# The head of a delta-rule attention and GELU layer kernel: norms, diagonals, joins, unread products and the order of loads

## The chip, the cores and the metric

The kernel runs on one core of one Trainium2 chip. The metric is device time in microseconds (us), lower is better. An engine is TensorE (PE in the profile; PEld is its weight load), VectorE (DVE), ScalarE (ACT), GpSimd (POOL) or SyncE (SP, here a queue that issues transfers). Each works through its own queue in order; semaphores join them.

## The reference

Two layers follow each other. The first is a delta rule, one state of 48 x 48 for each of 4 batches and 8 heads, over 768 tokens; the second is a dense layer with exact GELU over all 3072 tokens.

```python
k_n = k / (np.linalg.norm(k, axis=-1, keepdims=True) + 1e-06)
for t in range(S):
    kt, vt, bt = (k_n[:, :, t], v[:, :, t], beta[:, :, t, None])
    y[:, :, t] = np.einsum('bhd,bhde->bhe', q[:, :, t], state)
    v_old = np.einsum('bhde,bhd->bhe', state, kt)
    state = state + bt[:, :, :, None] * np.einsum('bhd,bhe->bhde', kt, vt - v_old)
...
x = np.ascontiguousarray(attn_out.transpose(0, 2, 1, 3)).reshape(B * S, H * D)
h = x @ w_in                                      # 3072 x 384 by 384 x 2048
g = 0.5 * h * (1.0 + erf(h / sqrt(2)))
out = g @ w_out                                   # 2048 x 384
```

The weights arrive as 64-bit floats and are rebuilt as 32-bit floats on the chip ("decoding").

## The kernel before

Tokens are taken in 12 chunks of 64. A tile is one chunk of two batches: 128 partitions hold two batches by 64 tokens, and 8 heads lie along the columns. So a chunk c has two tiles (a = 0, 1), and two chunks make a group g with four tiles (numbered t = 0 to 3). Inside a chunk the recurrence is a triangular system. Its matrix is the Gram matrix of the keys, scaled by beta over squared norms. Each 64 x 64 triangle is split into blocks of 32: the two diagonal blocks are inverted by elimination on VectorE, for all heads of a group at once, in thirty row steps (L515 to L530), and the lower left block follows from two small products, the joins (L568).

The head is the code from L201 to L1301. In it, the order of every engine is written out by hand:

- Keys of four tiles are loaded, squared and summed over columns (`squares`, L330), and turned by TensorE (`transposed`, L405), with a copy from PSUM to SBUF on ScalarE (the tile Kt).
- `diagonals` (L476) makes the two 32 x 32 diagonal blocks of each head: 32 products per tile, then one copy to the tile diag.
- `root` (L385) takes a square root on VectorE: a first guess from the bits, then three Newton steps of three operations. `factors` (L322) adds 1e-6, inverts, and makes beta over the squared norm (gm).
- `scales` and `flip` (L495, L506) turn gm and diag so that the row of a block lies along partitions; GpSimd multiplies gm by a triangular mask into the tile XM, and VectorE multiplies the flipped diag by XM (L513).
- While row steps run, TensorE and ScalarE do other preparation: Gram matrices of 16 products per tile (`grams`, L445), turned queries and their products (`queries`, L463), and the same for the third and fourth chunk.
- After the row steps, `back` (L536) turns the result three times: into XM, into the right half of Zf, and into the left half of Zf. `join` (L568) is called for each tile, level 0 (multiplied by gm into XM on VectorE) and level 1 (copied into Zf by ScalarE). `clear` (L552) zeroes the lower left parts of Zf.
- `solve`, `use`, `read`, `turn`, `update` and `next_state` (L779 to L885) compute the first chunk, whose outputs (xT) are what the dense layer multiplies: `fc1` (L909), 16 blocks f of 128 columns of w_in, three products and one GELU each.
- Decoding of one of the 16 weight parts n takes VectorE four or five operations on 768 columns: `begin` (L247: exponent bits), `mantissas` (L269, two operations), `signed` (L276: L281 and L282). Between, ScalarE turns exponent bits into a scale (`exponents`, L258): one Relu, or, where `two_kinks(n)` holds, two Prelus, and then VectorE needs no L281. Parts 0 to 7 are w_in, two blocks f each; parts 8 to 15 are w_out. `fetch` (L223) issues a part's loads; its raw bytes wait in four slots.

From L1316 on, steps get due times by hand (1.05 is 5% into the second unit of the plan) and are emitted in that order; a recording layer keeps VectorE and GpSimd in that order, and `together`, `behind` and `keep` fix parts of TensorE's and ScalarE's. SP issues all loads in the order in which they were written.

Of the kernel before, what the change touches and what calls it, by code (L numbers as in the profile page):

```python
# [19 lines left out]
def kernel(  # L20
# [31 lines left out]
    C = 64  # L52
# [33 lines left out]
    lim = cpool.tile([128, 4], F32)  # L86
    for i, x in enumerate((-896.0 * 2 ** 23, 0.0, -896.0 - 1792.0 / 4095.0, 128.0 * 1792.0 / 4095.0)):
        nc.vector.memset(lim[:, i:i + 1], x)
# [96 lines left out]
    Gp = [cpool.tile([128, NA, NF, 128], F32, name=f"G{i}") for i in range(2)]  # L185
    G = Gp[0]
# [18 lines left out]
    nc.scalar.activation(lim[:, 1:2], lim[:, 0:1], ACT.Gelu)  # L205
# [33 lines left out]
    def two_kinks(n):  # L239

        return 2 < n < n_in or n_in + 3 < n < n_in + 7
# [27 lines left out]
    def mantissas(n):  # L269
        dst, lo, hi, e = halves[n]  # L270
        bits = dst.bitcast(U32)
        nc.vector.tensor_scalar(bits, hi, 0xFFFFF, 0x100000, op0=ALU.bitwise_and,
                                op1=ALU.bitwise_or)
        nc.vector.scalar_tensor_tensor(dst, lo, 2.0 ** -32, bits, ALU.mult, ALU.add)

    def signed(n):  # L276

        dst, lo, hi, e = halves.pop(n)
        scale = high(e, BF16) if two_kinks(n) else e.bitcast(F32)
        if not two_kinks(n):  # L280
            nc.vector.scalar_tensor_tensor(e, hi, 0x80000000, e, ALU.bitwise_and, ALU.bitwise_or)  # L281
        nc.vector.scalar_tensor_tensor(dst, dst, 2.0 ** -20, scale, ALU.mult, ALU.mult)  # L282
        after = n + (NS if n < n_in else len(slots))
        if (after < n_in) == (n < n_in):
            fetch(after)

# [12 lines left out]
    def decode_in():  # L299

        marks = {3: (None, 1.05, 0.99, 1.06), 4: (1.0, 1.09, 1.1, 1.13),
                 5: (1.12, 1.18, 1.14, 1.2), 6: (1.19, 1.24, 1.21, 1.25),
                 7: (1.245, 1.3, 1.29, 1.36)}
        steps = []
        for n, (a, b, c, d) in marks.items():
            if a is not None:
                steps += [(a, (begin, n))]
            steps += [(b, (exponents, n, keep)), (c, (mantissas, n)), (d, (signed, n))]
        return steps
# [75 lines left out]
    def root(x):  # L385

        shape = list(x.shape)
        s = wk.tile(shape, F32, tag="root", name="root", bufs=1)
        r = wk.tile(shape, F32, tag="root_r", name="root_r", bufs=1)
        nc.vector.tensor_scalar(s.bitcast(U32), x.bitcast(U32), 0.5, 532487669.0,  # L390
                                op0=ALU.mult, op1=ALU.add)
        nc.vector.tensor_scalar_mul(x, x, 0.5)
        for i in range(3):
            nc.vector.reciprocal(r, s)
            nc.vector.tensor_tensor(r, r, x, op=ALU.mult)
            nc.vector.scalar_tensor_tensor(x if i == 2 else s, s, 0.5, r, ALU.mult, ALU.add)
# [8 lines left out]
    def transposed(u, part=(0, 1)):  # L405
        for x in part:
            if x == 0:
                dst = u.Kt = wk.tile([128, 2, NP, C], F32, tag="Kt", name="Kt", bufs=6)
            elif u.c == 1:
                dst = u.Qt = su.tile([128, 2, NP, C], F32, tag="Qt1", name="Qt1")  # L410
            else:
                dst = u.Qt = SQ[:, u.a, :, :, D:]
            if x and u.c == 3:
                psT = dn("psT")[:, 0].rearrange("q (j n) -> q j n", n=128)
            else:
                psT = sq("psT", NP, 128)
            flat = (Qp[2 + u.a] if u.c == 3 and x == 0 else (u.Kp, u.Qp)[x]).rearrange("q h d -> q (h d)")
            for j in range(NP):
                nc.tensor.transpose(psT[:, j, :], flat[:, j * 128:(j + 1) * 128], ident)
            nc.scalar.copy(dst.rearrange("q p j n -> q j p n"),  # L420
                           psT.rearrange("q j (p n) -> q j p n", p=2))
# [23 lines left out]
    def grams(us):  # L445
        g = us[0].c // 2
        psG = products(us, 0)
        if us[0].t == 0:
            Gs[g] = (wk if g else su).tile([128, NU, HB], F32, tag="G", name="G", bufs=1)
        span = slice(us[0].t * H, (us[-1].t + 1) * H)  # L450
        put = put_off if us[0].c > 5 else lambda name, dst, src: nc.scalar.copy(dst, src)
        put("gram", heads(Gs[g][:, span]), psG[:, :, :, HB:C])
        if g > 0:
            if us[0].t == 0:
                Ds[g] = wk.tile([128, NU, HB], F32, tag="diag", name="diag", bufs=1)
            put("gram", heads(Ds[g][:, span]), psG[:, :, :, 0:HB])
            for p in range(2):
                lower = slice(p * C + HB, (p + 1) * C)
                put("gram", Ds[g][lower, span], Gs[g][lower, span])

# [15 lines left out]
    def diagonals(u):  # L476

        if u.t == 0:
            Ds[0] = wk.tile([128, NU, HB], F32, tag="diag", name="diag", bufs=1)
# [11 lines left out]
    def eliminate_steps(g):  # L491
# [44 lines left out]
        def back(x):  # L536
# [4 lines left out]
            elif x == 1 or g == 0:  # L541
                cols = slice(HB, C) if x == 1 else slice(0, HB)
                nc.vector.transpose(Zf[g % 2][:, :, cols].rearrange("q u i -> q i u"), nu)
# [8 lines left out]
        def clear(g):  # L552
                for cc in range(2):
                    for p in range(2):
                        part = Zf[g % 2][p * C + HB:(p + 1) * C,
                                         cc * NU // 2:(cc + 1) * NU // 2, 0:HB]
                        if g == cc == p == 0:
                            nc.scalar.mul(part, low[0:HB, 0:HB // 2], 0.0)
                        else:
                            nc.gpsimd.memset(part, 0.0)  # L560

# [3 lines left out]
        steps += [(1.9, back, x) for x in range(3)]  # L565
        return steps + [(0.0, clear, 0)] if g == 0 else steps

    def join(g, ts, level, copy=nc.scalar.copy):  # L568
# [13 lines left out]
        for i in range(0, len(ts), 2):  # L582
            us = slice(ts[i] * H, (ts[min(i + 1, len(ts) - 1)] + 1) * H)
            n = us.stop - us.start
            for p in range(2):
# [6 lines left out]
                else:  # L592
                    copy(zf[top, us, HB:C], psJ[top, i // 2, 0:n])

# [314 lines left out]
    def fc1(c, f):  # L909
# [8 lines left out]
        if c <= 1 or f < EARLY:  # L918
            keep(nc.scalar.activation, *gelu)
        else:  # L920
            nc.scalar.activation(*gelu)
# [270 lines left out]
    def signs(c0, c1):  # L1192
# [7 lines left out]

    by_hand = ExitStack()
    by_hand.enter_context(tc.manual_schedule(engines={
        mybir.EngineType.DVE, mybir.EngineType.Pool, mybir.EngineType.Activation,
        mybir.EngineType.PE, mybir.EngineType.SP}))
    load_v(0)
    for n in range(2):
        fetch(n)
    load_k(2, "Kp")
    new_group(0)
    n0 = wk.tile([128, 2 * NA, H], F32, tag="n0", name="n0", bufs=1)  # L1210
    for c in range(2):
        ns[c] = n0[:, c * NA:(c + 1) * NA]
    for u in first:
        squares(u, n0[:, u.t], nc.gpsimd if u.t == 1 else nc.vector)
        transposed(u, (0,))
        if u.t in (1, 2):
            diagonals(first[u.t - 2 + 1])
# [3 lines left out]
    root(n0)  # L1221
    scales_, flip_, *rows, back0, back1, back2, clear_ = [s_[1:] for s_ in eliminate_steps(0)]
    factors(gms[0], beta_m[:, 0:2].rearrange("q c a h -> q (c a) h"), n0)
    scales_[0]()
    flip_[0]()
    ng = wk.tile([128, NA, H], F32, tag="ng", name="ng", bufs=1)
    for u in first:
        grams([u])
    signs(2, NC)
    third = [tiles[2, a] for a in range(NA)]  # L1230
    sums_ = [(u, h) for u in third for h in range(H)]
    for u in first:
        transposed(u, (1,))
        if u.c == 1:
            for x in sums_[5 * u.a:5 * u.a + 5]:
                sum_of_squares(*x)
        queries([u])
    for a in range(NA):
        fetch_q(tiles[2, a])
    for a in range(NA):  # L1240
        fetch_in(Qp[2 + a][:, :, 0:D], k, tiles[3, a])
    for n in range(2, NS):
        fetch(n)
    for n in range(n_in, n_in + 3):
        fetch(n)
    load_v(1)
    for u in third:
        transposed(u, (0,))
    for x in sums_[10:13]:
        sum_of_squares(*x)  # L1250
    grams(third)
    for u in third:
        transposed(u, (1,))
    for x in sums_[13:]:
        sum_of_squares(*x)
    fourth = [tiles[3, a] for a in range(NA)]
    for u in fourth:
        transposed(u, (0,))
    grams(fourth)
    for fn, *args in rows:  # L1260
        fn(*args)
    nc.vector.scalar_tensor_tensor(ng, gms[0][:, 0:NA], -1.0, ns[0], ALU.mult, ALU.mult)
    back0[0](*back0[1:])
    against_state(first[:NA])
    for u in first:
        masked(u)
    back1[0](*back1[1:])
    for a in range(NA):
        join(0, (a,), 0)
    back2[0](*back2[1:])  # L1270
    for a in range(NA):
        join(0, (a,), 1)
    clear_[0](*clear_[1:])
    for u in first[NA:]:
        scale_v(u)
    begin(0)
    exponents(0)
    mantissas(0)
# [30 lines left out]
    def state_at(c, *times, first=(), second=(), last=()):  # L1309

        steps = state_steps(c, first, second, last)
        if len(times) > len(steps):
# [7 lines left out]
    plan += [at(1.06, 1.065, [(1.0, load, 3)]),  # L1320
             [(t, (join, 0, range(NA, 2 * NA), level)) for level, t in enumerate((1.085, 1.16))],
# [20 lines left out]
    plan += [at(1.36, 1.361, [(1.0, fetch, n_in + 3)]), at(1.07, 1.071, [(1.0, load_v, 2)]), at(2.727, 2.728, [(1.0, sum_of_w, 1, 2)]), at(2.96, 2.961, [(1.0, last_sum_of_w)]), at(3.07, 3.071, [(1.0, sum_of_w, 4)])]  # L1342
# [129 lines left out]
```

## Time and profile before

| | |
|---|---|
| median of 3 runs | 625.69 us (625.04 to 627.02) |
| the profiled execution | 626.68 us, of which the span of instructions is 624.9 us |
| busy, share of the span | PE 96%, PEld 86%, DVE 70%, ACT 39%, POOL 34% |
| granted TensorE clock | 0.989 over the span; 0.50 from 44.48 to 58.13 us |
| row steps of the first group | 18.29 to 39.87 us, VectorE |
| first product of fc1 | 56.95 us |
| VectorE from 57 to 111 us | busy 14.11 of 15, 16.13 of 18, 20.59 of 21 us |
| row steps of the second group | 114.64 to 136.24 us, VectorE |

The profile is of one execution. A row of the timeline gives the start, the duration, the engine, the line and operation, output tile and input tiles with shapes, and in brackets the idle time before it and what ended it. "x4" counts instructions; TensorE's 32-bit products appear as two records each, its transposes as one. A row of the chain of waits gives start, duration and what carried the end; "issue" is time in which the profile shows nothing waited for. A row of the view by stages gives the busy time of each engine in a stretch, then the granted clock, the busy share of the transfer engines, and GB/s.

### The profile page before, as it was taken

How to read it: one execution, taken by the hardware profiler on the slowest of the kernel's cores; microseconds unless marked ns; L12 is line 12 of the kernel's file. 1: busy time of each engine (PE TensorE's matmuls, PEld its weight loads, DVE VectorE, ACT ScalarE, POOL GpSimd, SP SyncE). 2: the span in 40 equal slices, each digit the busy share in tenths (PEclk: the TensorE clock that was granted, in tenths of full speed). 3: DMA queues.
4: the chain of work that ended last, by engine and by line, in shares of the span. 5: the costliest groups of instructions: out<-in, count | busy, mean ns of one | idle time of the engine just before them, and what ended most of it. 6: DMA issues, size and time to landing. Idle time of an engine off the chain costs nothing.

```text
span 624.9 us, 19704 instructions
## 1 busy us (share of the span) xinstructions
PE 602.5 (96%) x8358; PEld 537.7 (86%) x8358; DVE 440.1 (70%) x811; ACT 241.4 (39%) x546; POOL 212.6 (34%) x316
## 2 busy tenths in 40 slices
PE   5768999999999999999999999999999999999997
PEld 4657786776899998998899998899998899988997
DVE  6999899999967697774859755859745947332532
ACT  3576877625443264224451134451134222044200
POOL 4045002100379821687222885222885200000000
PEclk9996999999999999999999999999999999999999
DMA  9793775002423452353123533013421001010011
GB/s 134 164 294 118 174 179 149 17 10 40 72 38 49 77 93 37 57 115 39 16 43 55 95 70 39 13 29 52 79 50 17 12 3 27 3 24 1 0 27 26
DMA packets 159576, 39.64 MB, mean 63 GB/s; under 512 B 151168, under 2 KB 154368, under 8 KB 159488
## 3 DMA queue, kind: packets, MB, share of 16 engines
q1 hardware_dynamic: 156816, 37.34, 30.9%
q10 hardware_dynamic: 2672, 1.03, 0.9%
q8 instruction: 66, 1.08, 0.7%
q14 instruction: 22, 0.18, 0.1%
HBM read 33.62 MB, written 4.72 MB: 61 GB/s over the span
## 4 chain that ended last, share of the span: by engine, by line
PE 81%; DVE 14%; issue 2%; DMA 1%; ACT 1%; SPq 0%; DVEq 0%
PE psX L966 13%; PE psY L1032 11%; PE psY L966 9%; PE psX L1032 9%; PE psV L1032 6%; PE psZ L1032 6%; PE psZ L966 4%; PE psV L966 4%; DVE tmp L528 3%; DVE Nu L530 3%; PE psK L732 3%; PE psO L933 3%; PE psH L915 2%; PE psY L822 2%; PE psU L792 2%
## 5 line engine op out<-in xcount | busy, mean ns | idle before, releaser
L377 POOL TENSOR_TENSOR n<-n,half 128x16 f32<-128x16 f32 x10 | 31.4, 3138 | 180.1 <-DVE n L375 130.0
L530 POOL TENSOR_TENSOR Nu<-Nu,tmp 128x30 f32<-128x30 f32 (+14 forms) x120 | 65.0, 541 | 9.4
L528 POOL TENSOR_TENSOR tmp<-Nu 128x30 f32<-128x30 f32 (+14 forms) x120 | 62.4, 520 | 9.4
L1032 PE MATMUL psX<-xT,w_in_sb 128*128 128x256 f32 (+1 forms) x288 | 62.6, 346 | 0.0
L966 PE MATMUL psX<-w_out_sb,G 128*128 128x192 f32 x320 | 56.1, 329 | 0.0
L966 PEld LDWEIGHTS psX<-w_out_sb,G 128*128 128x128 f32 x320 | 52.2, 190 | 0.7
L1032 PEld LDWEIGHTS psX<-xT,w_in_sb 128*128 128x128 f32 x288 | 47.9, 190 | 5.4
L915 PE MATMUL psH<-xT,w_in_sb 128*128 128x256 f32 x192 | 44.7, 387 | 0.7 <-ACT G L1015 0.5
L933 PE MATMUL psO<-w_out_sb,G 128*128 128x384 f32 x128 | 43.9, 490 | 0.0
L851 DVE TENSOR_TENSOR V<-psY,y 64x192 f32<-64x192 f32 (+1 forms) x60 | 21.3, 355 | 31.0 <-PE psY L834 27.0
L915 PEld LDWEIGHTS psH<-xT,w_in_sb 128*128 128x128 f32 x192 | 36.2, 192 | 7.9 <-ACT G L1015 2.3
L1060 DVE TENSOR_TENSOR psY<-psY,pu 128x512 f32<-128x512 f32 x20 | 14.0, 700 | 40.5 <-PE psY L1032 39.9
L1032 PE MATMUL psY<-xT,w_in_sb 128*128 128x256 f32 (+1 forms) x192 | 41.5, 345 | 0.0
L1015 ACT COPY xT<-psX 128x768 f32<-128x768 f32 x9 | 7.2, 799 | 79.8 <-PE psX L892 79.8
L1015 ACT COPY pu<-psZ 128x512 f32<-128x512 f32 x40 | 23.5, 587 | 37.3 <-PE psZ L1032 35.0
L933 PEld LDWEIGHTS psO<-w_out_sb,G 128*128 128x128 f32 x128 | 23.6, 190 | 14.1
L1032 PEld LDWEIGHTS psY<-xT,w_in_sb 128*128 128x128 f32 x192 | 32.1, 191 | 3.5
L1015 ACT ACTIVATE G<-G 128x512 f32<-128x512 f32 x40 | 25.2, 631 | 21.0 <-DVE G L1068 20.8
L1068 DVE TENSOR_TENSOR G<-psY,pu 128x512 f32<-128x512 f32 x20 | 13.8, 691 | 22.2 <-PE psY L1032 21.5
L1015 ACT ACTIVATE G<-psY 128x512 f32<-128x512 f32 x20 | 11.9, 596 | 45.3 <-PE psY L1032 45.3
L966 PE MATMUL psY<-w_out_sb,G 128*128 128x192 f32 x160 | 28.1, 329 | 0.0
L966 PE MATMUL psZ<-T,pu 128*128 128x192 f32 x160 | 28.1, 329 | 0.0
(207 smaller groups left out, 1370.2 us busy)
## 6 DMA issues: line engine op xcount, KB each, us to landing
Kp<-in_k_dram SPq DMA_DIRECT2D x76, 96.0 KB, 3.2
w_out_sb<-in_moe_w_in_dram SPq DMA_DIRECT2D x24, 256.0 KB, 4.0
V<-in_v_dram SPq DMA_DIRECT2D x48, 96.0 KB, 3.1
w_raw<-in_moe_w_out_dram SPq DMA_DIRECT2D x12, 384.0 KB, 7.4
out_dram<-o_sb SPq DMA_DIRECT2D x40, 96.0 KB, 2.2
Qp<-in_k_dram SPq DMA_DIRECT2D x64, 32.0 KB, 2.3
G<-in_moe_w_out_dram SPq DMA_DIRECT2D x4, 384.0 KB, 5.1
Qp<-in_q_dram SPq DMA_DIRECT2D x96, 16.0 KB, 2.0
```

Source lines behind the costliest of these rows:

```text
L377: nc.gpsimd.tensor_tensor(flat, flat, half, op=ALU.pow)
L528: rows_on.tensor_tensor(tmp, nu[:, j + 1:, j:j + 1].to_broadcast([128, n, j]), nu[:, j:j + 1, 0:j].to_broadcast([128, n, j]), op=ALU.mult)
L530: rows_on.tensor_tensor(nu[:, j + 1:, 0:j], nu[:, j + 1:, 0:j], tmp, op=ALU.add)
L732: nc.tensor.matmul(u.psK[HALF[p], r, j, :], lhsT=u.Kt[rows, p, j, :], rhs=SQ[rows, u.a, p ^ r, j, 0:w], start=True, stop=True)
L851: nc.vector.tensor_tensor(dst, src, pairs(u.y[at_], s), op=ALU.add)
L915: nc.tensor.matmul(psH, lhsT=w_in_sb[:, f // 2, m, f % 2 * 128:(f % 2 + 1) * 128], rhs=xTs[c][:, m, :], start=(m == 0), stop=(m == NM - 1))
L933: nc.tensor.matmul(u.psO, lhsT=G[:, u.a, f, :], rhs=w_out_sb[:, f, :], start=(f == 0), stop=(f == NF - 1))
L966: nc.tensor.matmul(ps_, lhsT=lhs[:, f, :], rhs=rhs[:, f, :], start=first and f == 0, stop=f == FH - 1, skip_group_check=not first)
L1015: i = fn(*args, **kw)
L1032: nc.tensor.matmul(ps_[:, i], lhsT=lhs[:, f // 2, f % 2 * 128:(f % 2 + 1) * 128], rhs=rhs, start=first and i == 0, stop=True, skip_group_c ...
L1060: nc.vector.tensor_tensor(L1["Y1"], L1["Y1"], L1["pu"][:, 0], op=ALU.add)
L1068: nc.vector.tensor_tensor(half(1, 1), shaped(L1["Y1"]), shaped(L1["pu"][:, 0]), op=ALU.add)
```

## The change

Nine edits, all in the head and in the few steps planned close behind it:

- **Root.** `root` and the first `factors` become `first_factors`: ScalarE takes Sqrt of n + 1e-30 and half of it plus 1e-6; VectorE adds one Newton step (four operations) and then the three operations that make gm. The Sqrt table is loaded first; the Gelu table is loaded behind the last diagonal's copy.
- **Diagonals.** Tiles 0 and 1 get `first_gram`: the full Gram matrix in 16 products, from which ScalarE copies diag and the Gram half, and GpSimd the lower diagonal blocks (four copies). Their separate Gram products later fall away. Tiles 2 and 3 keep `diagonals`.
- **Joins.** For the first chunk `join_first` computes two heads in one 64 x 64 product (16 products a level instead of 32). At level 1, ScalarE copies one batch's results and VectorE the other's.
- **Left half of Zf.** Two ScalarE copies (`upper_left`) for the first chunk, and two more, planned at 1.05, for the second, take the place of the third transpose on VectorE. GpSimd clears the lower left parts right after XM, in two operations.
- **Unread products.** `unread` multiplies zeros (the tile blank) into a PSUM tile that nothing reads: two of 512 columns first of all, one of 192 or 256 columns behind each of 13 row steps, two of 512 behind the last, 1280 columns between the two levels of the join, 256 behind.
- **Row steps as marks.** Preparation of the third and fourth chunk on TensorE is put behind row steps 9, 10, 12, 15 and 17 by semaphore (`behind_rows`). Sums of squares of the third chunk follow in one run on ScalarE.
- **Loads.** Keys and queries of the third and fourth chunk go ahead of V and weights, into tiles of their own (parts of G). The first three w_out raws are issued behind w_in's raws 4, 5 and 6 instead of in the head. `load(3)` and `load_v(2)` move from 1.06 and 1.07 to 1.1 and 1.12.
- **Decoding.** `two_kinks` holds for part 2 as well; `begin(0)` stands ahead of the level 1 copies.
- **Order.** All GELUs of `fc1` are kept in program order; marks in `decode_in` move by up to 0.03.

```diff
+    blank = G[:, 0, 8:12].rearrange("q f n -> q (f n)")
+    nc.vector.memset(blank, 0.0)
...
-    nc.scalar.activation(lim[:, 1:2], lim[:, 0:1], ACT.Gelu)
+    nc.scalar.activation(lim[:, 1:2], lim[:, 1:2], ACT.Sqrt)
...
-        return 2 < n < n_in or n_in + 3 < n < n_in + 7
+        return 1 < n < n_in or n_in + 3 < n < n_in + 7
...
+        if n < len(slots) - 1:
+            fetch(n_in + n)
...
+    def first_factors(gm, bt_, n):
+        s, t, r, h = (wk.tile(list(n.shape), F32, tag=x, name=x, bufs=1)
+                      for x in ("root", "root_t", "r", "root_h"))
+        nc.scalar.activation(s, n, ACT.Sqrt, bias=lim[:, 4:5], scale=1.0)
+        nc.scalar.activation(t, s, ACT.Copy, bias=1e-6, scale=0.5)
+        nc.vector.tensor_scalar_mul(h, n, 0.5)
+        nc.vector.reciprocal(r, s)
+        nc.vector.tensor_tensor(r, r, h, op=ALU.mult)
+        nc.vector.tensor_tensor(n, r, t, op=ALU.add)
+        yield
+        nc.vector.reciprocal(r, n)
+        nc.vector.tensor_tensor(gm, bt_, r, op=ALU.mult)
+        nc.vector.tensor_tensor(gm, gm, r, op=ALU.mult)
...
+    def first_gram(u):
+        psG = products([u], 0)
...
+        nc.scalar.copy(heads(Ds[0][:, span]), psG[:, :, :, 0:HB])
+        nc.scalar.copy(heads(Gs[0][:, span]), psG[:, :, :, HB:C])
+        for p in range(2):
+            lower = slice(p * C + HB, (p + 1) * C)
+            nc.gpsimd.tensor_copy(Ds[0][lower, span], Gs[0][lower, span])
...
+    def upper_left(us, put=lambda fn, *args: fn(*args)):
+        for p in range(2):
+            top = slice(p * C, p * C + HB)
+            put(nc.scalar.copy, Zf[0][top, us, 0:HB], Zf[0][top, us, HB:C])
...
+    def join_first(level):
...
+            for k in range(H):
+                us = slice(2 * k, 2 * k + 2)
+                nc.tensor.matmul(psJ[HALF[p], k, :], lhsT=(xm if level else off)[rows, us, :],
+                                 rhs=zf[rows, us, HB:C] if level else xm[rows, us, :],
+                                 start=True, stop=True)
...
+                    (nc.vector.tensor_copy if p else nc.scalar.copy)(
+                        zf[p * C:p * C + HB, us, HB:C], src)
...
+    def unread(*cols):
+        psI = ps.tile([128, 512], F32, tag="mlp", name="psI")
+        for n in cols:
+            m = min(n, 128)
+            nc.tensor.matmul(psI[0:m, 0:n], lhsT=blank[:, 0:m], rhs=blank[:, 0:n],
+                             start=True, stop=True)
...
+    def behind_rows(fn, *args):
+        after = latest(mybir.EngineType.DVE)
+        n = len(nc.cur_bb.bb.instructions)
+        fn(*args)
+        new = next(i for i in nc.cur_bb.bb.instructions[n:] if i.engine == mybir.EngineType.PE)
+        tc.add_manual_dep(new, after.name,
+                          mybir.DependencyInfo(mybir.DependencyClass.Sync,
+                                               mybir.DependencyReason.DATA), reason="time")
...
+    between = {9: [(turned, third, 0)], 10: [(grams, third)], 12: [(turned, third, 1)],
+               15: [(turned, fourth, 0)], 17: [(grams, fourth)]}
+    idle = {13: (256,), 14: (256,), 18: (256,), 19: (256,), 20: (256,), 21: (256,), 22: (256,), 23: (256,), 24: (256,), 25: (256,), 26: (192,), 27: (192,), 28: (256,)}
...
+    behind_rows(unread, 512, 512)
     back0[0](*back0[1:])
-    against_state(first[:NA])
-    for u in first:
+    against_state(first[:1])
+    for u in first[:3]:
         masked(u)
+    against_state(first[1:NA])
+    masked(first[3])
     back1[0](*back1[1:])
-    for a in range(NA):
-        join(0, (a,), 0)
-    back2[0](*back2[1:])
-    for a in range(NA):
-        join(0, (a,), 1)
-    clear_[0](*clear_[1:])
+    upper_left(slice(0, NA * H))
+    join_first(0)
+    unread(512, 512, 256)
+    begin(0)
+    join_first(1)
+    unread(256)
+    exponents(0)
+    mantissas(0, (0,))
+    mantissas(0, (1,))
```

## The prediction

> **What bounds the kernel now.** I read the page's slices first, then the chain of waits in order of time, the stages by window, and the timeline of the head (the first 60 us, all that the diff reaches).
>
> The page's line by engine:
>
> ```profile
> PE 81%; DVE 14%; issue 2%; DMA 1%; ACT 1%; SPq 0%; DVEq 0%
> ```
>
> TensorE carries the end and VectorE's 14% lies in front. From 138.58 us on the chain is TensorE without a hole over 1.1 us. What the head gains is therefore kept whole, if TensorE and VectorE both arrive that much earlier at 138 us, where TensorE waits 0.2 us for VectorE's XM (L539). The head, as the chain names it (start, duration, what):
>
> ```profile
> 13.63 0.90 PE psD L487 x46
> 14.55 0.38 ACT diag L489
> 14.95 1.98 DVE Nu L508
> 17.03 1.24 DVE Nu L513
> ...
> 40.00 2.16 DVE XM L539
> 42.15 1.81 DVE Zf L543
> 44.05 0.36 issue
> 44.41 0.43 DVE XM L589
> ...
> 45.76 1.93 DVE Zf L543
> 47.70 0.39 DVE w_e L255
> ```
>
> So: diagonals, flip, scaling, thirty row steps (18.3 to 39.9), three transposes around the joins, then decoding. VectorE is busy 14.1 of 15 us from 57 to 72 and 20.6 of 21 from 90 to 111.
>
> **The clock.** The view by stages cut where the granted clock changes (columns PE, PEld, DVE, ACT, POOL busy, then the clock):
>
> ```profile
> 34.24:44.48 10.24, 5.32 (x196) 4.49 (x188) 9.61 (x24) 8.13 (x25) 4.41 (x5) 1.00 0.98 352
> 44.48:58.13 13.65, 11.57 (x265) 10.15 (x266) 13.37 (x17) 9.43 (x22) 10.14 (x8) 0.50 0.45 100
> ```
>
> The joins' 1.20 us of small products are nearly all the work from 41.1 us to 44.48 us, and then the clock is 0.50 for 13.65 us. The view also says 1.00 before 34.24, but the timeline denies that:
>
> ```profile
> 4.47 1.09 PE L419 MATMUL psT<-ident,Kp 128*128 128x128 f32 x4 [4.47 <-DMA Kp<-in_k_dram]
> ...
> 34.95 1.09 PE L419 MATMUL psT<-ident,Qp 128*128 128x128 f32 x8
> ```
>
> Four transposes take at 4.5 us what eight take at 35: the head ran at half clock before 34 us, too.
>
> **Part 1: up to the row steps.** VectorE's sums of squares end at 9.66 in both. Now twelve operations (9.70 to 12.7: root and the addition of 1e-6) become two on ScalarE and four on VectorE. TensorE starts with two unread 512-column products on the cleared blank (ready at 1.4: 0.9 start plus 0.47 for 512 columns by the 0.70 row of 768). A 384-column record of L933 takes 0.33 at full clock, so 512 take 0.44; two records a product, two products: 1.75 at full, 3.5 at half. They end at 4.9, so the first transposes begin 0.5 late. The Gram of a tile (16 products instead of 32) replaces psD for tiles 0 and 1.
>
> Queue by queue, with copies Kt 0.59, diagonals and Gram halves 0.37, small ScalarE operations 0.24 (0.20 to 0.25 in rows of one column and of 48):
> - Clock still half: tile 3's transposes end 11.1, its Kt copy 11.75, Sqrt and half-root by 12.2; reciprocal 0.35, three short operations and a second reciprocal by 13.7; gt 0.21; POOL's XM 1.91 ends 16.0. The scaling starts at 16.05 instead of 17.03: 1.0 earlier.
> - Clock full from about 7 us: tile 3's Kt copy ends 10.3, roots 10.7, factors 12.3, gt 12.5, XM 14.6. The scaling starts at 14.67: 2.4 earlier. The four POOL copies of diagonals end by 10.6, before.
>
> The stall of 1.36 us inside psD (12.28 to 13.63, put down to "issue") sat on this path. It came after 119 products of TensorE's stream; the new stream has 116 up to the end of psD, so I expect it behind. Were it to fall inside, the start would move back by up to 1.4.
>
> I take the full clock: 3.5 us of dense 512-column work covers most of one 3.41 us window (the 13.65 us at 0.50 are four), and in the window to 34.24, after which the clock rose, TensorE was busy throughout. Against it: the window from 6.93 to 10.35 was busy throughout as well, with smaller tiles, and nothing rose. The Trainium skill (TensorE: Matmul & The Clock Gate, What's actually happening) says that one busy window of about 3.4 us releases the clock and one idle window takes it away; the first half would give the full-clock case, while the second half is contradicted here, as the longest hole before 44.48 is 2.06 us.
>
> POOL's two clearings of Zf (1024 columns each, about 1.2 by the 0.73 row of 512) now lie under the scaling and the first row steps. The nearest row is L272 under such a clearing at 48.0, 0.97 instead of 0.55: +0.42. Bounds 0 to 1.2; I take 0.45. The Trainium skill (SBUF — State Buffer, SBUF: two separate sides) has a two-input VectorE operation lock only against a GpSimd operation that reads; by that a clearing would cost nothing, and the sum would be 4.6 in place of 4.2. **Part 1: 1.9 us** (bounds 0 to 2.9).
>
> The Gelu table now loads behind the last diagonal (1.28 by its row): it delays Gram copies that nobody needs before 40 us. The row steps are the same instructions. Unread products wait for row steps; no row step waits for them. SP's queue carries third and fourth tiles' 16 loads ahead of V and raws: from 10.9 us by the rows 3.8 (four of k), 7.2 (eight of q), 2.6 (four of k), 3.7 (V), 3.5 (raws 0 and 1), so tile pair 4's k is issued by 24.6 and lands near 26.9, some 1 us after row step 15 asks for it (TensorE waits, VectorE does not); V by 28.3 and raws by 31.8 against first use at 40 and 46. The w_out raws, later, have until 78.
>
> **Part 2: joins and first decode**, in the old time, then shifted by part 1. XM and Zf transposes end at 43.95 as now. The unread 1.75 us after the last row ends at 41.8, before the joins' XM (42.15). The joined products end by 43.0, so XM L589 still runs 43.98 to 45.73 (four of 256 columns, 0.43 each, as before). Then the third transpose (1.93) goes; begin(0) takes 0.55 to 46.28, while psJ of level 1 (32 records, 0.6 by the Grams' 1.18 for 64) is ready at 46.55; two Zf copies of 256 columns from PSUM at 0.43 end at 47.41. Mantissas start there instead of 48.0: **0.6**.
>
> Rows of VectorE were stretched by POOL behind that:
>
> ```profile
> 50.34 1.19 DVE L272 TENSOR_SCALAR w_in_sb<-w_out_sb 128x768 uint32<-128x768 uint32 x1
> ...
> 51.56 1.47 DVE L274 SCALAR_TENSOR_TENSOR w_in_sb<-w_out_sb,w_in_sb 128x768 f32<-128x768 uint32 x1
> ```
>
> Normal are 0.55 and 0.96; with 0.97 at 48.0 the excess is 1.57. POOL now ends at 48.7 instead of 52.2 (its clearings, 2.18, are gone from here), so only mantissas(0) collide; 0.6 left: **1.0** gained (bounds 0.3 to 1.57).
>
> Part 2 of the weights gets two kinks: one L281, **0.95**, goes from VectorE; ScalarE pays 2.13 for two Prelus instead of 0.94. ScalarE also gets the second half's corner copies, 1.24. I lay its queue: xT by 54.1, Prelus 56.2, two gelus 57.0, corner copies 58.6; then weights 3's Prelus end 62.1, where VectorE is ready at 61.9: **-0.25**.
>
> TensorE at full clock: psU 1.15 instead of 2.3 us, then V copies, psY, x copies, xT as ScalarE's queue lets them (six copies of 0.97 a pair); fc1 begins at 54.2 instead of 56.95. It then waits for weights 1 (57.4 instead of 58.83) and for XM of the second half (64.5 instead of 66.8). So VectorE sets it there, and fc1 from its sixth column on moves by 2.3, as decoding does.
>
> **Sum:** 1.9 + 0.6 + 1.0 + 0.95 - 0.25 = 4.2 us. The profiled run took 626.68 (span 624.9, 1.8 around it) and would take 622.5; the median shown, 625.69, lies 0.99 lower, so the forecast is 621.5.
>
> **Rivals** (all against the median):
> - *The front stays at half clock.* For: the busy but small-tiled windows before 31 us. Part 1 is 1.0 - 0.45 = 0.55; the time 622.8.
> - *The clock falls again after 48 us.* There TensorE has only 48-column products paced by ScalarE, like the joins that lost it before. fc1's first two columns then take 2.7 more, of which 1.6 fit in its wait for XM; copies behind psU add little: 622.5.
> - *ScalarE takes it back.* The added 1.17 and 1.24 us lie just where gelus free fc1's two PSUM buffers (TensorE waited 0.5 on G there). If nothing covers them, 2.4 of the gain goes: 623.9.
> - *Slower: products of zeros don't hold the clock.* Then unread work only blocks TensorE's queue: 3.5 us to 43.5, joins 1.0, 4.4 us more, level 1 at 49.9, Zf at 50.9 instead of 47.4. psU follows at half clock and fc1 begins near 59.5. With five columns and two joins (9.2) and 2 us of half clock it reaches 70.7 instead of 68.0: 628.4. It decides from the point at which the unread stretch after level 0 outlasts XM's 1.75 us by over 2 us. Against it: nothing in the trace shows data mattering; for it, no zero product is in the trace.
>
> **Chances:** forecast (620.4 to 622.2) 0.49, front cold 0.20, clock falling 0.13, ScalarE 0.09, slower 0.06, more than forecast (part 1 at 2.9, all stretching gone: 619.5) 0.03. Range 619.4 to 624.3: it leaves out the slower case and tails of the others. A measurement of this kernel tells about 0.3% (1.9 us) from no change: faster by that 0.83, within 0.11, slower 0.06.
>
> **What would show it.** Eight transposes' pace at 7 us; the scaling's start (L513's form) near 14.7; the clock at 1.00 from 44 to 58; no third transpose and Zf ready at 45.4 (47.4 less part 1); rows of 0.55 and 0.96 in the first decode; fc1's start near 52. I am wrong if the granted clock drops where unread products stand, if a second issue stall falls in psD, or if TensorE shows idle time on G between 52 and 66.

## The result and the profile after

The changed kernel takes 628.12 us (median of 7 runs, 627.2 to 629.24) where the kernel before took 625.69 (7 runs beside them): 1.0039 times as long, 95% interval 1.0024 to 1.0053. It is 0.4% slower; the forecast was 4.2 us faster. The profiled execution took 629.08 us, of which the span is 627.4.

The page of the kernel after, time that carries the end by engine:

```profile
PE 87%; DVE 3%; ACT 2%; DMA 1%; issue 0%; SPq 0%; DVEq 0%
```

VectorE's share fell from 14% to 3% and TensorE's rose from 81% to 87%: the chain no longer runs through the second group's row steps. Where it leaves TensorE is told by the same chain in order of time (start, duration, what):

```profile
96.41 0.97 DVE w_out_sb L293
97.38 0.37 SPq L243
...
97.80 6.46 DMA w_raw<-in_moe_w_out_dram
...
104.36 0.57 DVE w_e L261
104.96 0.94 ACT w_e L267
...
107.35 4.34 PE psH L961 x12
```

A load of a w_out raw of 6.46 us now stands in the chain, behind its issue on SP's queue. VectorE, ScalarE and then TensorE follow it: TensorE stands idle for 3.15 us before 107.35, waiting for G. Before, the chain held no load between 62 and 130 us.

VectorE's waits from 40 to 139 us say the same (total, times, longest; the kernel before had no wait on a load there):

```profile
DVE w_e L261 <- DMA w_raw<-in_moe_w_out_dram: 2.6, 2, 1.9
DVE w_in_sb L293 <- ACT w_e L1058: 2.5, 2, 2.3
DVE Zf L638 <- ACT Zf L638: 2.0, 1, 2.0
DVE w_e L264 <- DMA G<-in_moe_w_out_dram: 1.3, 1, 1.3
...
DVE w_e L261 <- DMA w_out_sb<-in_moe_w_in_dram: 0.5, 1, 0.5
```

These are late raws (2.6 + 1.3 = 3.9 us for the w_out parts 13, 14 and 15, and 0.5 for one of w_in), ScalarE's late exponents (2.3 in one wait) and the first join (2.0). A table of how far VectorE is ahead of the kernel before at six of its rows (start before minus start after, positive is ahead) puts them in order; the last two columns are experiments told below.

| VectorE's row | before at | after | raws in the head | and join in two tiles |
|---|---|---|---|---|
| scaling of the diagonals | 17.03 | +2.70 | +2.69 | +2.71 |
| transpose into XM behind the row steps | 39.99 | +2.69 | +2.69 | +2.73 |
| mantissas(0) | 48.00 | +0.64 | +0.63 | +1.47 |
| state of the first chunk (SQ) | 58.86 | +2.20 | +2.20 | +3.03 |
| XM of the second half | 65.40 | +1.17 | +1.32 | +4.03 |
| gt of the second group | 111.20 | -3.11 | +1.45 | +3.66 |

Each column is one execution, and the front alone differs between executions: raws_late, an experiment below whose head before the row steps is that of the kernel before, scales at 16.27 instead of 17.03. The level of a column is uncertain by that much; its steps from row to row are surer. Read down the third column: the front gains 2.7 us, the joins lose 2.06, the first decode gains 1.56, ScalarE takes 1.03 net, and between 65 and 111 us 4.3 us go.

**The front** did what was forecast, and more. TensorE's rows of the kernel after:

```profile
7.46 0.65 PE L434 MATMUL psT<-ident,Kp 128*128 128x128 f32 x4
...
13.67 1.97 PE L455 MATMUL psG<-Kt 48*64 48x64 f32 x58 [2.46 <-issue]
```

Four transposes take 0.65 us where they took 1.11 at the same place before: behind the unread products the clock is up. The issue stall (2.46 us) fell behind the diagonals, into Gram products that nobody waits for yet, and VectorE scales at 14.33. It stands behind 220 records of TensorE's stream, as the stall before does, so the prediction's way of placing it, by a count of products, was right.

**The clock** by stages (columns as before):

```profile
12.99:19.82 6.83, 6.15 (x110) 5.25 (x114) 6.06 (x16) 2.65 (x6) 3.19 (x3) 0.50 0.56 96
19.82:47.13 27.31, 24.73 (x374) 17.47 (x370) 23.39 (x56) 17.54 (x58) 9.70 (x9) 1.00 0.65 167
47.13:57.37 10.24, 10.12 (x201) 8.60 (x195) 9.97 (x15) 7.83 (x18) 1.63 (x1) 0.50 0.41 128
```

The full clock of the front is lost again from 12.99 to 19.82 us, the time of the stall and behind it, where VectorE waits for nothing of TensorE's. The half clock at the joins now begins at 47.13 and lasts 10.24 us, not 13.65 from 44.48. It still covers the first chunk's products and the first columns of fc1.

**The joins**, from the timeline of the kernel after:

```profile
39.54 1.87 PE L624 MATMUL psJ<-XM,G 32*64 32x64 f32 x32
41.34 2.42 PE L1249 MATMUL psI<-G 128*128 128x512 f32 x6
...
45.67 0.75 ACT L638 COPY Zf<-psJ 32x256 f32<-32x256 f32 x2 [3.17 <-PE psJ L624]
46.45 0.88 DVE L638 COPY Zf<-psJ 32x256 f32<-32x256 f32 x2 [2.05 <-ACT Zf L638]
```

Sixteen two-head products (32 records) take 1.87 and 1.90 us at full clock, against 1.20 for the 64 records of one head each before. The unread 1280 columns end at 43.76, behind XM (43.18). And VectorE's two copies begin only when ScalarE's two end, which the profile names as the end of their wait; both read one PSUM tile.

**SP's queue** around the late raws, after:

```profile
53.07 0.91 SPq L243 DMA_DIRECT2D w_raw<-in_moe_w_out_dram  x2
...
90.40 0.87 SPq L243 DMA_DIRECT2D w_raw<-in_moe_w_out_dram  x2
...
94.42 1.96 SPq L243 DMA_DIRECT2D w_raw<-in_moe_w_out_dram  x2
...
97.18 1.04 SPq L243 DMA_DIRECT2D w_raw<-in_moe_w_out_dram  x2
```

and before:

```profile
35.17 4.76 SPq L234 DMA_DIRECT2D w_raw<-in_moe_w_out_dram  x6
40.44 3.69 SPq L100 DMA_DIRECT2D V<-in_v_dram  x4
53.95 8.11 SPq L234 DMA_DIRECT2D w_out_sb<-in_moe_w_in_dram  x9
...
85.47 0.87 SPq L234 DMA_DIRECT2D w_raw<-in_moe_w_out_dram  x2
...
89.98 1.67 SPq L234 DMA_DIRECT2D w_raw<-in_moe_w_out_dram  x2
...
93.71 0.80 SPq L234 DMA_DIRECT2D w_raw<-in_moe_w_out_dram  x2
```

The raws of parts 12, 13 and 14 are issued 4.9, 4.4 and 3.5 us later, although VectorE is ahead at that point. The reason lies further up in the queue. Before, raws 8 to 10 were issued from 35.17 on, in 4.8 us, loads of V behind them until 44.1, and SP then had nothing to issue until 53.95. After, they are issued at 53.07, 56.99 and 60.18, ahead of the fourth chunk's keys and queries (the last query loads start at 73.15 instead of 69.95) and of the blocks of keys (80.75 instead of 77.25). From 55 to 70 us the loads move 325, 396 and 270 GB/s in stretches of 5 us (before 211, 280 and 219), and from 45 to 50 us only 3.

### The profile page after: what moved, and what is told of

Read it like the earlier page. It is cut to its first block, busy times and chain, and to the rows that moved or that the text cites. A ratio compares the mean times of both kernels' runs of the same rounds, so it can differ in the third digit from the quotient of the medians.

```text
span 627.4 us, 19435 instructions
## 1 busy us (share of the span) xinstructions
PE 612.6 (98%) x8208; PEld 540.8 (86%) x8208; DVE 437.1 (70%) x805; ACT 244.8 (39%) x552; POOL 213.3 (34%) x323
## 3 DMA queue, kind: packets, MB, share of 16 engines
q10 hardware_dynamic: 2672, 1.03, 0.8%
q8 instruction: 64, 1.05, 0.7%
## 4 chain that ended last, share of the span: by engine, by line
PE 87%; DVE 3%; ACT 2%; DMA 1%; issue 0%; SPq 0%; DVEq 0%
PE psX L1009 12%; PE psY L1075 11%; PE psY L1009 9%; PE psX L1075 8%; PE psH L961 6%; PE psV L1075 6%; PE psZ L1075 6%; PE psO L976 5%; PE psV L1009 4%; PE psZ L1009 4%; PE psK L778 3%; PE psY L868 2%; PE psU L838 2%; PE psQ L798 2%; PE psJ L697 1%; PE psG L455 1%
## 5 line engine op out<-in xcount | busy, mean ns | idle before, releaser
L390 POOL TENSOR_TENSOR n<-n,half 128x16 f32<-128x16 f32 x10 | 29.8, 2984 | 189.2 <-DVE n L388 130.1
L961 PE MATMUL psH<-xT,w_in_sb 128*128 128x256 f32 x192 | 47.0, 400 | 4.0 <-ACT G L1058 4.0
L1009 PE MATMUL psY<-T,G 128*128 128x192 f32 x160 | 28.1, 329 | 0.0
```

The costliest lines, as they stand in the source:

```text
L390: nc.gpsimd.tensor_tensor(flat, flat, half, op=ALU.pow)
L961: nc.tensor.matmul(psH, lhsT=w_in_sb[:, f // 2, m, f % 2 * 128:(f % 2 + 1) * 128], rhs=xTs[c][:, m, :], start=(m == 0), stop=(m == NM - 1))
L1009: nc.tensor.matmul(ps_, lhsT=lhs[:, f, :], rhs=rhs[:, f, :], start=first and f == 0, stop=f == FH - 1, skip_group_check=not first)
```

## The experiments

The theory is that the moved w_out raws cost more than everything else gains. Its rival is that the head's gain was lost in the head already (joins, clock, ScalarE), and that the waits on raws only show what TensorE would have waited for anyway. Line numbers differ by a few between kernels.

### The raws alone, from both sides

The changed kernel with raws 8 to 10 issued in the head again (raws_head):

```diff
...
-        if n < len(slots) - 1:
-            fetch(n_in + n)
...
     for n in range(2, NS):
         fetch(n)
+    for n in range(n_in, n_in + 3):
+        fetch(n)
```

> The changed kernel, but the first three w_out raws are issued in the head again, behind w_in's raws 2 and 3. Theory A (the raws, moved into the stretch from 53 us on where loads already fill the queues, make weight parts 12 to 15 late): VectorE's waits on raws near 100 to 109 us (3.9 us in the changed kernel) and TensorE's 3.1 us on G there go, and the time falls by 3 to 4.5 us to about 624. Theory B (the loss is ScalarE's added work and the clock at 0.50 from 47 us, and the late loads only follow from that): the time stays within 1 us of 628.1 and the waits remain.

Measured: 623.86 us, 0.996 (0.9947 to 0.9974).

The kernel before with only this order changed the other way (raws_late, the same lines moved from the head into `signed`):

> The kernel before with one edit: the first three w_out raws are issued behind w_in's raws 4, 5 and 6, as in the change. Theory A: waits on raws appear in the w_out decode and the kernel is 3 to 4.5 us slower than before, about 629.5. Theory B: within 1 us of 625.7.

Measured: 631.69 us, 1.0077 (1.0053 to 1.0101). VectorE's waits on w_out raws there, from 40 to 139 us (1.3 us on a w_in raw come on top):

```profile
DVE w_e L252 <- DMA w_raw<-in_moe_w_out_dram: 1.8, 2, 1.4
DVE w_e L255 <- DMA G<-in_moe_w_out_dram: 1.4, 1, 1.4
```

The order of three raws costs (1.0039 - 0.996) x 626 = 4.9 us in the changed kernel and 4.8 in the kernel before, and with it come and go the waits on loads. The theory holds. The column "raws in the head" of the table is the same as "after" until 65 us, and then keeps its 1.3 us. But raws_head gains 2.5 us, not 4.2: the head does lose some of its own. Of the 6.6 us between forecast and measurement the raws are 4.9, and the head 1.7.

### Does the queue or the amount of transfers do it?

Two kernels on the fast variant of the next section (join in two tiles, raws in the head). In split_loads, load(3) and load_v(2) go back to their old times:

```diff
...
-    plan += [at(1.1, 1.105, [(1.0, load, 3)]),
+    plan += [at(1.06, 1.065, [(1.0, load, 3)]),
...
-at(1.12, 1.121, [(1.0, load_v, 2)])
+at(1.07, 1.071, [(1.0, load_v, 2)])
```

> The fastest kernel so far with load(3) and load_v(2) back at their old times, 1.06 and 1.07. If the transfers between 50 and 70 us matter only through the raws, 622.0 with nothing moved on VectorE. If the later loads are needed once the raws stand in the head, VectorE waits on a w_in raw near 73 us or TensorE on V, and it is 1 us or more slower.

Measured: 629.08 us, 1.0039 (1.0021 to 1.0056), 7 us behind the kernel that it was made from. One wait of VectorE:

```profile
DVE w_e L261 <- DMA w_out_sb<-in_moe_w_in_dram: 7.0, 1, 7.0
```

SP's queue of split_loads shows why:

```profile
69.83 2.66 SPq L105 DMA_DIRECT2D V<-in_v_dram  x4
72.58 2.67 SPq L243 DMA_DIRECT2D w_out_sb<-in_moe_w_in_dram  x3
```

and that of the kernel it was made from (join_split):

```profile
59.68 1.30 SPq L243 DMA_DIRECT2D w_out_sb<-in_moe_w_in_dram  x3
```

The same bytes are moved in both, but a w_in raw stands behind the fourth chunk's loads and V instead of ahead of them: issued at 72.58 instead of 59.68. So here it is the place in the one queue that counts; for the three raws the issue times above say the same, and no run changes the amount alone. (The profiled execution took 632.13 us, the longest of its twelve.) The second half of my expectation was right, the first wrong: the later times of these loads, which the prediction passed over as well, are a needed part of the change (decoding's marks had moved later by up to 0.03, past 1.06).

split_late is the changed kernel with only the join in two tiles; its raws stay late:

> The changed kernel with only the join's products of the two batches put into two PSUM tiles; the first three w_out raws stay behind w_in's raws 4 to 6. If the raws' price is VectorE waiting for bytes whose issue times hang on SP's queue, a faster front gives nothing of that back, since VectorE then only arrives earlier at the same late bytes: the split's 1.85 us shrink to 0 to 1, the time is 627 to 628, and VectorE's waits on the raws grow from 3.9 us to about 5. If the two costs are independent (the raws' lateness moves with the head), it is 626.3 with 3.9 us of waits. If the split alone had carried what the kernel with raws in the head gained, it is near 622.

Measured: 627.77 us, 1.0024 (1.0007 to 1.0042). The 2.1 us that the same edit gives when the raws are early (below) shrink to (1.0039 - 1.0024) x 626 = 0.9, with intervals that overlap. VectorE's waits on loads are 3.5, 2.2 and 0.4 us, in an execution of 630.28 us, the longest of its twelve. This speaks for the first case: who comes earlier waits longer for the same bytes.

### The joins

join_split is raws_head with the two batches' products in two PSUM tiles:

```diff
...
-        psJ = dn("psJ")[:, 0].rearrange("q (k n) -> q k n", n=2 * HB)
+        psJs = [t.rearrange("q (k n) -> q k n", n=2 * HB) for t in (dn("psJ")[:, 0], sq("psJ", 512))]
...
-                nc.tensor.matmul(psJ[HALF[p], k, :], lhsT=(xm if level else off)[rows, us, :],
+                nc.tensor.matmul(psJs[p][HALF[p], k, :], lhsT=(xm if level else off)[rows, us, :],
...
```

> As the kernel with the raws in the head; the joined products of the two batches go to two PSUM tiles, so that VectorE's copies into Zf no longer wait for ScalarE's. If that wait (2.1 us behind begin(0), of which about 0.8 is ScalarE's two copies) is what the join lost against the forecast: VectorE's copies end 0.8 us earlier (46.5 instead of 47.3) and the time falls by about 0.8. Rival: the 1.9 us of products of level 1 set it; then Zf is ready no more than 0.2 earlier and the time is the same.

Measured: 622.01 us, 0.9927 (0.9915 to 0.9938): the best kernel together with split_short below, and (0.996 - 0.9927) x 626 = 2.1 us better than raws_head. Its timeline at the join:

```profile
43.63 1.90 PE L622 MATMUL psJ<-Zf,XM 32*64 32x64 f32 x32
44.87 0.75 ACT L636 COPY Zf<-psJ 32x256 f32<-32x256 f32 x2 [2.42 <-PE psJ L622]
45.62 0.88 DVE L636 COPY Zf<-psJ 32x256 f32<-32x256 f32 x2 [1.26 <-ACT Zf L636]
```

ScalarE now copies the first batch while TensorE makes the second, and VectorE begins 0.09 us behind the last product: 0.83 us earlier than after. ScalarE's copies end at the same 45.62, so whether VectorE would still wait for them can't be seen here. More is gained with the clock, which the view by stages shows at 1.00 here, and so on to the end:

```profile
45.00:50.00 5.00, 4.82 (x140) 3.55 (x137) 4.25 (x8) 4.13 (x12) 4.08 (x3) 1.00 0.83 329
```

With it, fc1 begins at 52.97 (55.19 in raws_head), VectorE's wait on exponents shrinks from 2.1 to 0.4 us, and it is 4.03 us ahead at the second half's XM.

How the 2.1 us divide between copies and clock stays open, since the clock is not the same in every execution of one kernel. raws_head's twelve runs fall into two groups: five of 622.31 to 622.80 us with a mean granted clock of 0.992 to 0.994, and seven of 623.44 to 626.13 us with 0.985 or 0.986, among them the profiled one. Against the first group (median 622.57) the two tiles gain only 0.56 us; in which stretch its clock held, runs without a profile don't show.

split_short takes from join_split the first 512 of the unread columns between the two levels:

> The fastest kernel so far (two PSUM tiles, raws in the head) with 768 instead of 1280 unread columns between the two levels of the join. They ended 0.5 us after XM, so if they only block the queue, level 1 starts at 43.2 instead of 43.63 and the kernel gains 0.3 to 0.5: 621.6. If they are what holds the clock through the joins, it falls to 0.50 near 47 again, and the kernel is back near 623.9.

Measured: 621.82 us, 0.9921 (0.9895 to 0.9947), no difference from join_split. In the profiled execution the clock was 1.00 from 45 to 55 us without them: it needed these columns as little as they cost anything that can be measured.

old_joins is raws_head with the first chunk's joins by single heads, as before the change, and ScalarE's copies:

```diff
...
-    join_first(0)
+    for a in range(NA):
+        join(0, (a,), 0)
     unread(512, 512, 256)
     begin(0)
-    join_first(1)
+    for a in range(NA):
+        join(0, (a,), 1)
```

> As the kernel with the raws in the head, with the first chunk's joins as in the kernel before: 32 products a level on 32 columns (1.20 us at full clock before), copies all on ScalarE (four of 0.37). If two heads in one 64 x 64 product are slower than four single ones (1.87 against 1.20 us), level 1 ends 0.7 us earlier on TensorE and Zf is ready no later than now: equal to 0.8 us faster. If joining two heads pays: 0.5 us or more slower.

Measured: 627.61 us, 1.0012 (0.9999 to 1.0024), and the runs lie far apart (624.73 to 629.87). In the profiled execution (626.05) its products take 1.20 us a level, and VectorE is 3.54 us ahead at the state, more than in any other kernel, 2.73 at XM and 2.87 at gt. So single heads are quicker at the join itself, and yet the kernel ends later than raws_head. What takes it behind 111 us, and what spreads it, stays open: the waits show issue stalls of TensorE at other places (1.4 us in the first chunk's psY), but no run here ties the time to them.

### The clock and ScalarE

hold is raws_head with more unread products among the first chunk's (512, then 1024, then 256 columns, and 1024 behind the join instead of 256), to keep the clock up from 46 to 55 us:

```diff
...
     solve(first[:NA])
+    unread(512, own=False)
     use(first[:NA])
+    unread(512, 512, own=False)
...
```

> As the kernel with the raws in the head, with more unread products: 1024 columns instead of 256 behind level 1, 512 behind psU, 1024 behind psY, 256 behind the first update. If the clock falls at 47 us for want of dense products, it stays at 1.00 until 57, psU takes 1.15 instead of 2.1 us, fc1 starts 0.7 to 1.5 us earlier than at 55.19, VectorE's 2.1 us wait for part 3's exponents shrinks, and the time falls by 0.7 to 2 us. If the time there is set by ScalarE's copies and VectorE's decoding whatever the clock: same within 0.5.

Measured: 624.47 us, 0.9968 (0.9956 to 0.998). The clock stayed at 1.00 from 45 us on, but fc1 began at 55.72 instead of 55.19 us; 0.41 of that lies ahead of the joins (the transpose into XM starts at 37.71 instead of 37.30). What the clock gave, the unread products took from TensorE's queue, which works in order.

raws_head_kinks is raws_head with part 2 of the weights on one Relu again (`return 2 < n < n_in`):

> As the kernel with the raws in the head, but weight part 2 is decoded with one Relu again. If ScalarE's queue takes back what the second Prelu gives (VectorE waits 2.3 us for part 3's exponents in the changed kernel), this is as fast or up to 1 us faster than the kernel with the raws in the head alone. If VectorE's 0.95 us are what counts, it is 0.5 to 1 us slower.

Measured: 624.08 us, 0.9965 (0.9951 to 0.998), the same time. VectorE's longest wait on exponents is 0.3 us instead of 2.1, but L281's 0.95 is back, so that it comes 0.81 us earlier to the second half's XM (63.27 instead of 64.08). So in raws_head the wait takes more from VectorE than the second Prelu gives. But the clock was also up sooner in this execution (0.59 from 50 to 55 us and 1.00 from there, against 0.50 and 0.79), and why nothing of the 0.81 us shows at the end stays open.

all_three joins the last two and join_split:

> The kernel with the raws in the head, two PSUM tiles for the joined products, the additional unread products, and weight part 2 with one Relu. If the three causes are separate, the gains add: 1.5 to 3 us less than with the raws in the head alone, 621 to 622.4. If VectorE's decoding sets the stretch alone, only the join's 0.8 is seen: 623.

Measured: 624.53 us, 0.997 (0.996 to 0.998), worse than join_split alone. fc1 begins at 55.73 instead of 52.97: hold's products and the one Relu together cost 2.7 us here, more than the two tiles gained. Which of them cost how much, this run doesn't tell.

no_unread is the changed kernel without any unread product:

> The changed kernel without any unread product; the other steps stay behind their row steps. If unread products lift the clock in front (theory A): half clock until 20 us or later, row steps start 1.0 to 1.7 us later than at 15.59, level 1 of the join about as late as now since 1280 columns in front of it go (0.5 earlier) while the clock there may be halved; in all 0 to 2 us slower, 628 to 630. If they only block TensorE's queue (rival): 0.5 to 1 us faster.

Measured: 631.29 us, 1.0086 (1.0065 to 1.0107). Its front and its clock:

```profile
8.05 1.11 PE L434 MATMUL psT<-ident,Kp 128*128 128x128 f32 x4
...
30.07:60.79 30.72, 19.54 (x333) 17.21 (x332) 25.05 (x51) 17.24 (x60) 11.29 (x9) 0.50 0.50 148
```

Four transposes take 1.11 us again, the scaling begins at 16.27 instead of 14.33, and the clock is 0.50 for 30.7 us. Products of zeros do raise and hold the clock; together, less what they cost in TensorE's queue, they are worth (1.0086 - 1.0039) x 626 = 2.9 us.

## Why the prediction was wrong

- **Failed: "The w_out raws, later, have until 78."** Costed at nothing, it cost 4.9 us. The sentence asked when the moved raws themselves are used, and they did come in time. What I left out is what stands behind them on SP's queue: the fourth chunk, V, the blocks of keys, and the raws of parts 12 to 15, whose issue moved back by up to 4.9 us. Those parts are decoded one behind the other from 95 to 113 us, with VectorE on the path that sets the end. The trace of before had the row for it: SP's queue stood empty from 44.1 to 53.95 us, and was in use almost without a break from there to 95. The change took three loads from ahead of the empty stretch and put them behind it.
- **Front, forecast 1.9, measured 2.7.** The full-clock case came true with its mechanism: transposes at 0.65, stall behind the diagonals, scaling at 14.33 (forecast 14.67). Part of the 2.7 is the length of the stall in the one profile before (1.36 us): in raws_late, with the same stream there, the stall is 0.27 and the scaling starts at 16.27, against which the front gains 1.9. The 0.45 for GpSimd's clearings was not paid: they ran from 14.35 to 16.28 over the scaling, which took its usual 1.23. The Trainium skill (SBUF — State Buffer, SBUF: two separate sides) lets a two-input VectorE operation be held only by a GpSimd operation that reads; this trace agrees.
- **Joins, forecast +0.6, measured -2.06.** Three terms of my sum failed. Products of level 1 were to take 0.6 us "by the Grams' 1.18 for 64"; they took 1.90. The copies were to run side by side on two engines; in the kernel after, they follow each other, for 0.8. And the unread columns ran 0.58 us past XM.
- **Stretching, forecast 1.0, measured 1.56**, the upper bound: rows of 0.55 and 0.96. The clearings were gone, and GpSimd's products into V, which before ran from 50.08 to 52.22 over the rows of 1.19 and 1.47, now ended at 45.88, ahead of the mantissas. `begin(0)` was stretched instead, under GpSimd's operations (1.19 at 43.22); it lies in the wait for the join and costs nothing.
- **L281 and ScalarE, forecast 0.95 - 0.25, measured -1.03 together** in the kernel after, and 4.03 - 3.03 = +1.00 where the clock held. This is the rival "the clock falls again after 48" and the rival "ScalarE takes it back", in one: the Prelus of part 3 (61.08) stood behind gelus that waited for fc1's first columns at half clock, and behind the corner copies of the second half (1.23 at 59.42).
- **The sum.** With the raws back in the head and the join mended, the same change gains (1 - 0.9927) x 626 = 4.6 us, near the 4.2 of the sum, but by other terms: 2.7, then 1.47 - 2.73 = -1.3 for the joins, 1.56 and 1.00 make 4.0 at the second half's XM.
- **The slower rival** (zeros don't hold the clock, 628.4) gave nearly the measured time by a wrong mechanism: zeros do hold it, as no_unread shows. That its number is close is luck.
- **Signs.** Of the three signs of being wrong, one came: the clock dropped at 47.13, 0.9 us behind unread columns. No stall fell into psD, and TensorE's waits for G came only behind 66 us. The upper case of the chances (619.5) adds up to 619.9 by its own terms.

## What to carry to other kernels

When a load is moved, don't ask when its own bytes are needed, but which loads stand behind it in its queue, and whether the place it leaves was idle: three loads put from ahead of an idle stretch into a busy one, still in time themselves, cost 4.9 us, and an order that is right for one plan cost 7 us in another. Give each engine that reads a joint result a PSUM tile of its own, so that the first can start while the products of the second are made. In a change of several parts, measure first the part that was costed at nothing.

## What the runs showed of the hardware

- The clock fell at 47.13 us although TensorE had no hole over 0.5 us in the 3.4 us before (its rows there: the joins, unread products, psU). The Trainium skill (TensorE: Matmul & The Clock Gate, What's actually happening) has one idle window take the full clock away; here it fell without one, as at 44.48 before, where the longest hole that lies whole in the 3.4 us ahead is 1.25 us. In the profiled executions it held near 47 in all five kernels with two tiles and fell there in all three with one tile and the same unread products. One execution of each doesn't show that the two tiles hold it: join_split and split_short have the same stream up to the joins, and from 20 to 30 us the clock is 1.00 in one and 0.50 in the other.
- Joining two heads in one 64 x 64 product of depth 32 halves the number of products and lengthens the stage: 32 records in 1.87 us (58 ns each) against 64 records in 1.20 us (19 ns each). The size of the output is not the reason: the Grams' products, also 64 x 64 but of depth 48, take 0.69 us for 32 records (22 ns each, in the row at 8.04 us after). What is, no run here shows.
- The first issue stall of TensorE keeps its place in the stream, not in time: in all thirteen profiles it stands behind exactly 220 of TensorE's records, whatever they are (in psD before and in raws_late, in Gram products in the others). Its length does not keep: 1.36 us at 12.28 before, 0.27 in raws_late, 2.46 at about 11.2 after, and 2.99 at about 11.3 in join_split, at no cost in the last two. The kernel before and raws_late have a second one 128 records further (0.60 and 1.16 us). What ends there, no run here shows.
